# LSH attention and two mixture layers on one core: the attention result's halves added on GpSimd, v stored by partition, a new order

## The chip, the cores and the metric

One core of a Trainium2 chip runs the whole program in one launch. The metric is the device time in microseconds (us) of that launch. The core's engines are PE (TensorE: matrix products and transposes), DVE (VectorE), ACT (ScalarE) and POOL (GpSimd); SP (SyncE) here only issues transfers. Each engine works through its own instructions in the order in which the program lists them.

## What is computed

The reference, cut to what matters. There are 2 x 8 heads of 768 positions and 64 channels; the result of the attention (1536 x 512) goes through two further layers, all in float32.

```python
q_bucket = bits of (q @ proj > 0), 6 bits; k_bucket likewise
scores = q @ k.T / 8, and -1e9 where q_bucket != k_bucket
attn = exp(scores - max);  attn = attn / (sum + 1e-9)
x = attn @ v                        # heads side by side: 1536 x 512
x = ((x @ w1) * (x @ w2)) @ w3 @ w_out
p = domain_probs / (sum + 1e-9)
out = sum over 4 experts e of p[:, e] * (relu(x @ e1[e]) @ e2[e])
```

## The kernel before, in words

Every float32 operand of a product is split into a high and a low part of a narrower type (hi and lo), and three or four products of parts take the place of one.

**Attention.** The work is 48 units u: 16 heads hh of 3 blocks of 256 queries each. For a head, `head` loads q and k (`ld`), scales and splits them on POOL (`sc`, `h`, `l`; for the first two heads on ACT and DVE), and sends pieces between partitions by transfers issued from SP (`k1`, `k2`, `k3`, `dq`). `lv` loads v, `vh` and `vl` split it on POOL. `pair` (and `first_head` for head 0) makes the mask bits: a product on PE (`bm`), a comparison on DVE, and transfers `mq` and `mk` that put them beside q and k.

A unit (`unit`) goes through every engine: scores of two blocks of 128 queries on PE (`S`); minimum with its copy out of PSUM on DVE (`mx`); exponential on ACT (`ex`); sum plus 1e-9 on POOL (`r1`), reciprocal on DVE (`r2`), scaling on POOL, one in four on ACT (`en`); then three groups of four transposes on PE (`T`), each copied out as a high part by ACT (`hi`) and a low part by DVE (`lo`); then twelve products with v on PE (`pv`) into one bank, pv_ps. Its 128 partitions hold two halves of 64 (products with the high and with the low part of v) that are to be added. Before the change ACT copies the lower half into `pvs` (`po`, line 502) and DVE adds it to the upper half in PSUM (`xa`, line 504) into xt, and the next unit's `pv` may then begin.

**Weights.** Weights come in 64-bit words. `conv64` (line 176) loads one, ACT and DVE turn it to float32 and split it; the first 8 pieces run beside the attention, with the last steps on POOL.

**The first product in attention.** The product of x's first 512 rows with w1 and w2 has 8 column tiles `ff` of twice 12 products. FILL of them (4 before) are put into gaps of PE in the late attention (`fm`; from unit UF = 38 on they have the bank `f_ps`, one group of twelve uses s_ps). After `switch` the memory is given to the later layers, and the rest of the first product and everything else run on PE as one long row of products (`u_ps`, `o_ps`).

**What sets the order.** No loop sets it. Each step is an `op` with an engine, an assumed duration in ns, the steps it waits for and a priority; `emit_all` plays a list scheduler over these: when an engine falls free in its model it takes the ready op with the smallest priority, and a finished op reaches another engine after LAT. Priority is the due time plus RANK of the group times 5500. The order that comes out is written as each engine's instruction list. The chip runs these lists with its own durations, and every list in order: an instruction whose input is late holds up all behind it on that engine. For SP the assumed duration stands for a transfer's place on the queue, and LAT of SP for its landing.

Of the kernel before, what the change touches and what calls it, by code (L numbers as in the profile page):

```python
# [14 lines left out]
ALU = mybir.AluOpType  # L15
# [11 lines left out]
    "CP": 16.1,  # L27
    "S0": -59.56,
    "S1": 3.69,
    "T0": -207.42,  # L30
    "T1": -82.6,
    "T2": -31.6,
    "b0": -57.56,
    "b1": -59.96,
    "bits": -7.65,
    "en": 2.75,
    "ex0": -95.56,
    "ex1": -444.49,
    "fd": -89.32,
    "fx": 240.7,  # L40
    "hi0": -7.87,
    "hi1": -248.41,
    "hi2": -157.19,
    "ld": -54.46,
    "lo0": -345.82,
    "lo1": -186.61,
    "lo2": -153.95,
    "lv": -53.81,
    "mx0": -264.79,
    "mx1": -0.59,  # L50
    "p0": -157.78,
    "p1": -422.6,
    "po": -405.44,
    "prep": 73.11,
    "pv": -5.01,
    "r1": -199.11,
    "r2": -270.42,
    "v": 180.48,
    "xa": -317.88,
}  # L60
# [11 lines left out]
def tile_lsh_attention_moe(ctx, tc, qk, v, projc, w1, w2, w3T, w_out, dp, e1, e2, out):  # L72
# [15 lines left out]
    def tiles(n, shape, name, dtype=F32, p=None):  # L88
        return [(p or ap).tile(shape, dtype, name=f"{name}{i}") for i in range(n)]
# [7 lines left out]
    NE_SLOTS = 4  # L97
    FILL = 4
    slots = [const.tile([128, 2, 1024], F32R, name=f"slot{i}") for i in range(NE_SLOTS)]
# [78 lines left out]
    def conv64(n, dst, half, src):  # L178
        r = raws[n % NRAW]

        def hi_():
            return slots[dst][:, 0, half * 512:(half + 1) * 512]

        def lo_():
            return slots[dst][:, 1, half * 512:(half + 1) * 512]

        ri = r.bitcast(I32)
        lw, hw = (ri.rearrange("p (a b) -> p a b", b=2)[:, :, i] for i in range(2))
        c, t = cbuf[:, n % NCB, 0], cbuf[:, n % NCB, 1]
        beside = n < NBESIDE  # L190
        side, sdur, seng, minus = ("POOL", 1225, nc.gpsimd, pool_lo) if beside else ("DVE", 620, nc.vector, lo_of)
        return [
            ("SP", 1460, [("cd", n - NRAW), ("c2", n - NRAW)], "cl",
             lambda: nc.sync.dma_start(out=ri.rearrange("p (a b) -> p a b", a=src.shape[1]), in_=src)),
            ("ACT", 520, [("cl", n), ("cq", n - NCB)], "ca",
             lambda: nc.scalar.activation(out=f(c), in_=f(hw), func=AF.Abs)),
            ("DVE", 335, [("ca", n)], "c0",
             lambda: nc.vector.tensor_scalar(out=f(c), in0=f(c), scalar1=EXP_LO, scalar2=EXP_HI, op0=ALU.max, op1=ALU.min)),
            ("DVE", 335, [("c0", n)], "c1",
             lambda: nc.vector.tensor_scalar(out=t, in0=c, scalar1=3, scalar2=0x3FFFFFFF, op0=ALU.logical_shift_left,  # L200
                                             op1=ALU.bitwise_and)),
            ("DVE", 602, [("c1", n)], "c2",
             lambda: nc.vector.scalar_tensor_tensor(out=c, in0=hw, scalar=-0x40000000, in1=t, op0=ALU.bitwise_and,  # L203
                                                    op1=ALU.bitwise_or)),
            ("DVE", 335, [("c2", n)], "c3",
             lambda: nc.vector.tensor_scalar(out=t, in0=c, scalar1=-0x800000, scalar2=None, op0=ALU.bitwise_and)),  # L206
            ("ACT", 520, [("c2", n)], "ch",
             lambda: nc.scalar.activation(out=hi_(), in_=f(c), func=AF.Copy)),
            (side, sdur, [("ch", n)], "cp", lambda: minus(lo_(), f(c), hi_())),
            ("DVE", 602, [("c3", n)], "cd",  # L210
             lambda: nc.vector.scalar_tensor_tensor(out=f(t), in0=lw.bitcast(U32), scalar=2.0 ** -52, in1=f(t),  # L211
                                                    op0=ALU.mult, op1=ALU.mult)),
            (side, sdur, [("cp", n), ("cd", n)], "cq",
             lambda: seng.tensor_tensor(out=lo_(), in0=f(lo_()), in1=f(t), op=ALU.add)),
        ]
# [17 lines left out]
    def conv(n, dst, half, src):  # L233
# [95 lines left out]
    def head(hh):  # L329
# [10 lines left out]
        def load(part):  # L340
            nc.sync.dma_start(out=r[part], in_=qk[b, h, part])
# [4 lines left out]
        def scaled_lo(eng):  # L346
            eng.scalar_tensor_tensor(out=lo, in0=r, scalar=svec, in1=f(hi), op0=ALU.mult, op1=ALU.subtract)
# [12 lines left out]
        else:  # L360
            op(("ld", hh), "SP", 1130, lambda: load(slice(0, 2 * D)), [("l", hh - RR)] if hh >= RR else [],
               -1e9 + 1e7 * hh if first else T - 8000)
            if first:
                op(("h", hh), "ACT", 733, lambda: nc.scalar.activation(out=hi, in_=r, func=AF.Copy, scale=svec),
                   [("ld", hh), ("sv", 0)], T, g)
# [6 lines left out]
            op(("k1", hh), "SP", 700, lambda: copy(ka[q], hi[k]), [("h", hh)] + old, T, g)  # L372
            op(("k3", hh), "SP", 700, lambda: copy(kb[q], hi[k]), [("h", hh)] + old, T, g)
            op(("k2", hh), "SP", 700, lambda: copy(ka[k], lo[k]), [("l", hh)] + old, T, g)
            op(("dq", hh), "SP", 700, lambda: copy(hi[k], hi[q]),
               [("bm", hh // 2 if hh > 1 else 0), ("k1", hh), ("k3", hh)], T, g)
# [45 lines left out]
    def unit(u):  # L422
# [6 lines left out]
        for t in range(2):  # L429
# [22 lines left out]
        def norm(t):  # L452
# [43 lines left out]
        Tp = T + 2.0 * P  # L496
        pvs = pvs_t[u % 2]
# [401 lines left out]
```

## Time and profile before

| | |
|---|---|
| median of 3 runs | 1017.81 us (1017.12 to 1022.36) |
| the profiled execution: its own time | 1020.02 us |
| its span, first to last instruction | 1018.2 us |
| busy: PE, DVE, ACT, POOL | 999.7, 510.1, 362.5, 307.8 us |
| bytes moved | 64.12 MB in 51135 packets, 17688 of them under 512 B |

The busy share of PE is 98%, but the profile models the ends of products, which overlap, so a busy PE is not PE at its peak. The span falls into two: the attention, in which all four engines work and hand on to one another, and what follows, in which PE runs products back to back. An engine that is nearly always busy in a stretch bounds it; an average over the span says nothing of that, so the prediction reads the stretches apart.

### The profile page before, as it was taken

What the parts mean: (1) busy time and instruction counts of PE and PEld (TensorE: products, weight loads), DVE (VectorE), ACT (ScalarE), POOL (GpSimd) and SP (SyncE); (2) the same over time, 40 slices, a digit from 0 to 9 for tenths busy, and PEclk for the clock granted to TensorE, in tenths of its full rate; (3) what the DMA queues carried; (4) which work ended last, traced back from release to release, by engine and by line L of the source; (5) the groups of instructions that cost most, each with busy time, mean ns of one, the idle gap of its engine ahead of it and who ended that gap; (6) DMA issues with size and microseconds to landing.
All of it is one profiled execution on the core that took longest, in us unless ns stands there. A gap on an engine that the chain in (4) does not pass through costs nothing.

```text
span 1018.2 us, 13166 instructions
## 1 busy us (share of the span) xinstructions
PE 999.7 (98%) x5035; PEld 844.6 (83%) x5035; DVE 510.1 (50%) x948; ACT 362.5 (36%) x669; POOL 307.8 (30%) x351
## 2 busy tenths in 40 slices
PE   7899999999999999999999999999999999999998
PEld 6888888988788888888888888888888888888886
DVE  6889999998599965954312212121121212212122
ACT  5889999988433322432201101101101101101100
POOL 6777788664000000074300064000650005300000
PEclk9999999999999999999999999999999999999999
DMA  6843544320034321332200032000220002001011
GB/s 162 184 128 77 130 121 112 82 80 21 1 116 127 119 94 49 117 103 63 63 1 1 1 93 73 0 1 1 78 88 1 1 1 73 31 1 42 1 42 42
DMA packets 51135, 64.12 MB, mean 63 GB/s; under 512 B 17688, under 2 KB 34072, under 8 KB 51072
## 3 DMA queue, kind: packets, MB, share of 16 engines
q1 hardware_dynamic: 50928, 63.27, 22.0%
q8 instruction: 40, 0.66, 0.3%
q14 instruction: 23, 0.19, 0.1%
q10 hardware_dynamic: 144, 0.01, 0.0%
HBM read 47.22 MB, written 3.15 MB: 49 GB/s over the span
## 4 chain that ended last, share of the span: by engine, by line
PE 82%; DVE 14%; DMA 1%; ACT 1%; issue 1%; POOL 1%; SPq 0%; DVEq 0%; ACTq 0%; POOLq 0%
PE u_ps L147 43%; PE o_ps L147 30%; DVE et L485 5%; DVE e L443 5%; PE s_ps L147 3%; PE pv_ps L147 2%; PE t_ps L477 2%; PE t_ps L147 2%; DVE xa L504 1%; DVE cbuf L211 1%; DMA wraw<-in_w 1%; ACT e L446 1%; DMA kb<-hh 0%; DVE cbuf L203 0%; DVE cbuf L206 0%
## 5 line engine op out<-in xcount | busy, mean ns | idle before, releaser
L819 DVE SCALAR_TENSOR_TENSOR hl<-u_ps,hl 128x512 fp32r<-128x512 f32 x96 | 66.4, 691 | 420.4 <-ACT hl L817 420.4
L817 ACT ACTIVATE hl<-u_ps 128x512 fp32r<-128x512 f32 x96 | 57.4, 598 | 459.3 <-PE u_ps L147 401.9
L147 PE MATMUL u_ps<-xh,slotl 128*128 128x512 f32 x936 | 220.6, 389 | 0.0
L147 PEld LDWEIGHTS u_ps<-xh,slotl 128*128 128x128 f32 x936 | 175.7, 188 | 36.5
L147 PE MATMUL u_ps<-xh,slot 128*128 128x512 f32 x696 | 165.0, 389 | 1.2 <-DVE xh L156 1.2
L147 PE MATMUL o_ps<-slotl,hl 128*128 128x512 f32 x648 | 154.7, 389 | 0.0
L147 PEld LDWEIGHTS u_ps<-xh,slot 128*128 128x128 f32 x696 | 130.6, 188 | 28.7 <-DVE xh L156 1.6
L147 PEld LDWEIGHTS o_ps<-slotl,hl 128*128 128x128 f32 x648 | 121.6, 188 | 25.2
L147 PE MATMUL o_ps<-slot,hl 128*128 128x512 f32 x504 | 119.9, 389 | 0.0
L147 PEld LDWEIGHTS o_ps<-slot,hl 128*128 128x128 f32 x504 | 94.6, 188 | 19.6
L159 POOL TENSOR_SCALAR slot<-wraw 128x512 fp32r<-128x512 f32 x28 | 17.8, 634 | 286.7 <-PE u_ps L147 269.7
L485 DVE TENSOR_TENSOR et<-t_ps,et 128x512 fp32r<-128x512 f32 x144 | 96.6, 680 | 5.8 <-ACT et L483 5.2
L446 ACT ACTIVATE e<-e,sm 128x768 f32<-128x768 f32 x96 | 89.5, 933 | 12.3 <-DVE e L443 11.0
L147 PE MATMUL pv_ps<-et,vv 128*128 128x256 f32 x576 | 92.8, 297 | 0.8 <-DVE xa L504 0.5
L443 DVE TENSOR_SCALAR_CACHE_REDUCE e<-s_ps 128x768 f32<-128x768 f32 x96 | 90.4, 945 | 4.9 <-PE t_ps L477 3.0
L477 PE MATMUL t_ps<-ident,e 128*128 128x128 f32 x576 | 87.0, 279 | 5.7 <-DVE et L485 4.0
L483 ACT ACTIVATE et<-t_ps 128x512 fp32r<-128x512 f32 x144 | 83.0, 592 | 12.5 <-PE t_ps L477 5.7
L159 POOL TENSOR_SCALAR slotl<-wraw 128x512 fp32r<-128x512 f32 x36 | 22.5, 624 | 208.8 <-PE u_ps L147 172.3
L477 PEld LDWEIGHTS t_ps<-ident,e 128*128 128x128 f32 x576 | 66.3, 142 | 15.9 <-DVE et L485 8.5
L147 PEld LDWEIGHTS pv_ps<-et,vv 128*128 128x128 f32 x576 | 76.0, 192 | 3.0 <-DVE xa L504 2.4
L456 POOL TENSOR_SCALAR e<-e,sm 128x768 f32<-128x768 f32 x72 | 65.5, 916 | 17.4 <-DVE sm L461 15.4
L147 PE MATMUL s_ps<-ka,hh 128*128 128x512 f32 x192 | 53.5, 360 | 3.8 <-issue 2.2
(111 smaller groups left out, 1092.9 us busy)
## 6 DMA issues: line engine op xcount, KB each, us to landing
wraw<-in_e SPq DMA_DIRECT2D x64, 256.0 KB
wraw<-in_w SPq DMA_DIRECT2D x16, 512.0 KB
wraw<-in_w3T SPq DMA_DIRECT2D x16, 512.0 KB
r<-in_qk SPq DMA_DIRECT2D x15, 384.0 KB
wraw<-in_w_out SPq DMA_DIRECT2D x8, 512.0 KB
rv<-in_v SPq DMA_DIRECT2D x16, 192.0 KB
out<-xa SPq DMA_DIRECT2D x12, 256.0 KB
ka<-hh SPq DMA_DIRECT2D x15, 192.0 KB
```

The source lines that it names most:

```text
L147: nc.tensor.matmul(out=o, lhsT=l, rhs=r, start=start, stop=stop)
L159: nc.gpsimd.tensor_scalar(out=o, in0=i, scalar1=1.0, scalar2=1.0, op0=ALU.mult, op1=ALU.mult)
L211: lambda: nc.vector.scalar_tensor_tensor(out=f(t), in0=lw.bitcast(U32), scalar=2.0 ** -52, in1=f(t), op0=ALU.mult, op1=ALU.mult)),
L443: op(("mx", u, t), "DVE", 873, lambda ps=ps, m=m, e=e: nc.vector.tensor_scalar(out=e, in0=ps[:, 0:S], scalar1=THR, scalar2=None, op0=ALU.m ...
L446: op(("ex", u, t), "ACT", 921, lambda e=e, m=m, rs=rs: nc.scalar.activation(out=e, in_=e, func=AF.Exp, scale=-1.0, bias=m, accum_out=rs), ...
L456: return "POOL", 872, lambda: nc.gpsimd.tensor_scalar(out=e, in0=e, scalar1=r[:, t:t + 1], scalar2=1.0, op0=ALU.mult, op1=ALU.mult)
L477: nc.tensor.transpose(out=ps[:, k, t * 128:(t + 1) * 128], in_=e_t[2 * (u % ER) + t][:, kt * 128:(kt + 1) * 128], identity=ident)
L483: op(("hi", n), "ACT", 480, lambda ps=ps, et=et: nc.scalar.activation(out=et[:, 0], in_=ps, func=AF.Copy), [("T", u, j), ("pv", n - NET)], Tj)
L485: op(("lo", n), "DVE", 602, lambda ps=ps, et=et: nc.vector.tensor_tensor(out=et[:, 1], in0=ps, in1=f(et[:, 0]), op=ALU.subtract), [("hi", ...
L504: op(("xa", u), "DVE", 340, lambda: nc.vector.tensor_tensor(out=xt[a, h // 2, t0:t0 + 256], in0=pv_ps[0:D], in1=pvs, op=ALU.add), [("po", ...
L817: op(("gh", n), "ACT", 480, lambda n=n, nu_=nu_: nc.scalar.activation(out=hl_t[n % 2][:, 0], in_=u_ps[nu_ % 4], func=AF.Relu), [ku] + hfre ...
L819: op(("uf", nu_), "DVE", 602, lambda n=n, nu_=nu_: nc.vector.scalar_tensor_tensor(out=hl_t[n % 2][:, 1], in0=u_ps[nu_ % 4], scalar=0.0, in ...
```

## The change

Five things change, all of them within the attention, and the order with them.

- `po` copies all 128 partitions of pv_ps into `pvs` (three buffers now). A transfer from SP (`pm`, new) puts one half of it into `pvd` on the partitions of the other half, and POOL, no longer DVE, adds the two (`xa`). The next unit's `pv` waits for `po`, no longer for `xa`.
- v lies in memory with 1.5 KB in a row for a partition, so that its load is 128 rows of 1.5 KB and no longer 768 of 256 B.
- For head 0 the comparison for q is cut in two: 256 columns, which unit 0 needs, then the other 512 (`sf`). `l` of head 1 now waits for the first of these.
- FILL is 2, no longer 4.
- All values of RANK are new, assumed durations are changed (transfers of weights 2700, no longer 1460; of q and k 2000, no longer 1130; copies 1000, no longer 700; conversions some 15% longer), and LAT of SP is 1900, no longer 2300. The load of head 2 also waits for the copies of head 0.

```diff
 RANK = {
...
-    "b0": -57.56,
+    "b0": -203.5,
...
-    "mx0": -264.79,
-    "mx1": -0.59,
-    "p0": -157.78,
-    "p1": -422.6,
-    "po": -405.44,
+    "mx0": -137.39,
+    "mx1": -120.26,
+    "p0": -518.7,
+    "p1": -224.16,
+    "pm": -94.42,
+    "po": -345.53,
...
-    "xa": -317.88,
+    "xa": -90.07,
 }
...
-    FILL = 4
+    FILL = 2
...
-    pvs_t = tiles(2, [64, 256], "pvs")
+    pvs_t = tiles(3, [128, 256], "pvs")
+    pvd_t = tiles(2, [128, 256], "pvd")
...
-            ("SP", 1460, [("cd", n - NRAW), ("c2", n - NRAW)], "cl",
+            ("SP", 2700, [("cd", n - NRAW), ("c2", n - NRAW)], "cl",
...
-        "SP": {"PE": 2300, "ACT": 2300, "DVE": 2300, "POOL": 2300, "SP": 2300, "NONE": 0},
+        "SP": {"PE": 1900, "ACT": 1900, "DVE": 1900, "POOL": 1900, "SP": 1900, "NONE": 0},
...
-            op(("ld", hh), "SP", 1130, lambda: load(slice(0, 2 * D)), [("l", hh - RR)] if hh >= RR else [],
+            op(("ld", hh), "SP", 2000, lambda: load(slice(0, 2 * D)), [(x, hh - RR) for x in (("l", "k1", "k2", "k3", "dq") if hh == RR else ("l",))],
...
-                op(("l", hh), "DVE", 870, lambda: scaled_lo(nc.vector), [("h", hh)], T, g)
+                op(("l", hh), "DVE", 1000, lambda: scaled_lo(nc.vector), [("h", hh), ("mq", 0)], T, g)
...
-        op(("lv", hh), "SP", 600, lambda: nc.sync.dma_start(out=rv, in_=v[b, h].rearrange("(k p) d -> p k d", p=128)),
+        op(("lv", hh), "SP", 1000, lambda: nc.sync.dma_start(out=rv, in_=v[b, h].rearrange("p (k d) -> p k d", k=NK)),
...
-        op(("mq", 0), "DVE", 865, lambda: is_pos(lo[64:64 + PC], ps, q), [("mk", 0)], T, "b0")
-        keys[("sf", n)] = keys[("mq", 0)]
+        for i, (key, c) in enumerate(((("mq", 0), slice(0, 256)), (("sf", n), slice(256, S)))):
+            op(key, "DVE", (330, 600)[i], lambda c=c: is_pos(lo[64:64 + PC, c], ps, q, c), [("mk", 0)], T + i, "b0")
...
-            op(("pv", n), "PE", 472, lambda j=j: pv(j), [("lo", n), ("vl", hh), ("xa", u - 1), ("pv", n - 1)], Tp)
+            op(("pv", n), "PE", 472, lambda j=j: pv(j), [("lo", n), ("vl", hh), ("po", u - 1), ("pv", n - 1)], Tp)
...
-        op(("po", u), "ACT", 264, lambda: nc.scalar.activation(out=pvs, in_=pv_ps[D:2 * D], func=AF.Copy),
-           [("pv", NJ * u + NJ - 1), ("xa", u - 2)], Tp)
-        op(("xa", u), "DVE", 340, lambda: nc.vector.tensor_tensor(
-            out=xt[a, h // 2, t0:t0 + 256], in0=pv_ps[0:D], in1=pvs, op=ALU.add), [("po", u)], Tp)
+        w, t0 = h % 2, b * S + qp * 256
+        a, o = slice(w * D, (w + 1) * D), slice((1 - w) * D, (2 - w) * D)
+        op(("po", u), "ACT", 283, lambda: nc.scalar.activation(out=pvs, in_=pv_ps, func=AF.Copy),
+           [("pv", NJ * u + NJ - 1), ("xa", u - 3)], Tp)
+        op(("pm", u), "SP", 500, lambda: nc.sync.dma_start(out=pvd[a], in_=pvs[o]), [("po", u), ("xa", u - 2)], Tp)
+        op(("xa", u), "POOL", 520, lambda: nc.gpsimd.tensor_tensor(
+            out=xt[a, h // 2, t0:t0 + 256], in0=pvs[a], in1=pvd[a], op=ALU.add), [("pm", u)], Tp)
```

## Rows read from the trace of the kernel before

**Rows 1.** Windows view: span, then PE, PEld, DVE, ACT, POOL busy (instructions), clock, DMA share, GB/s.
```profile
50.00:250.00 200.00, 194.21 (x1376) 175.72 (x1375) 193.39 (x408) 181.06 (x358) 145.34 (x174) 0.99 0.39 96
...
262.70:272.96 10.26, 10.26 (x45) 8.18 (x44) 1.11 (x2) 3.73 (x8) 0.00 (x0) 1.00 0.00 0
272.96:1018.20 745.24, 740.30 (x3265) 612.50 (x3263) 269.75 (x441) 135.60 (x228) 124.30 (x128) 1.00 0.15 49
```

**Rows 2.** Groups of instructions of DVE, 50 to 250 us: busy us, mean ns, idle before.
```profile
L485 DVE TENSOR_TENSOR et<-t_ps,et 128x512 fp32r<-128x512 f32 x120 | 80.5, 679 | 2.7 <-ACT et L483 2.3
L443 DVE TENSOR_SCALAR_CACHE_REDUCE e<-s_ps 128x768 f32<-128x768 f32 x80 | 75.4, 945 | 1.3 <-PE s_ps L147 0.9 <-PE t_ps L477 0.4
L504 DVE TENSOR_TENSOR xa<-pv_ps,pvs 64x256 f32<-64x256 f32 x40 | 16.5, 412 | 1.4 <-ACT pvs L502 0.7
L211 DVE SCALAR_TENSOR_TENSOR cbuf<-wraw,cbuf 128x512 f32<-128x512 uint32 x8 | 8.4, 1055 | 0.0
```

**Rows 3.** The last step of the weight conversion, whole span: ns min/median/max.
```profile
L211 DVE SCALAR_TENSOR_TENSOR cbuf<-wraw,cbuf x40: 672/692/1440, 60.9 to 434.8; 128x512 f32<-128x512 uint32 x40
```

**Rows 4.** Groups of instructions of POOL, 50 to 250 us.
```profile
L162 POOL TENSOR_TENSOR ll<-r,hh 128x768 fp32r<-128x768 f32 x10 | 18.4, 1840 | 0.7
L162 POOL TENSOR_TENSOR vv<-rv,vv 128x384 fp32r<-128x384 f32 x13 | 13.2, 1013 | 0.9
...
L159 POOL TENSOR_SCALAR vv<-rv 128x384 fp32r<-128x384 f32 x13 | 6.6, 510 | 4.5 <-PE pv_ps L147 4.2
```

**Rows 5.** Groups of instructions of ACT, two copies that differ in partitions alone.
```profile
L358 ACT ACTIVATE hh<-r,svec 64x768 fp32r<-64x768 f32 x1 | 0.9, 936 | 1.4 <-POOL ka L162 1.4
L352 ACT ACTIVATE hh<-r,svec 128x768 fp32r<-128x768 f32 x1 | 0.9, 935 | 0.1
```

**Rows 6.** Waits in 50 to 250 us: total, times, longest.
```profile
PEld pv_ps L147 <- DVE xa L504: 2.1, 4, 0.8
```

**Rows 7.** Timeline of the start: start us, us, what, idle before.
```profile
6.03 2.60 POOL L162 TENSOR_TENSOR ka<-r,hh 64x768 fp32r<-64x768 f32 x1 [4.24 <-ACT hh L352]
...
7.28 2.17 DVE L347 SCALAR_TENSOR_TENSOR ll<-r,svec,hh 128x768 fp32r<-128x768 f32 x1 [0.34 <-ACT hh L364]
...
7.57 0.28 PE L147 MATMUL s_ps<-ll,pbh 128*128 128x256 f32 x1
...
9.48 1.07 DVE L394 TENSOR_SCALAR kb<-s_ps,thr,amp 12x768 fp32r<-12x768 f32 x1
...
10.59 1.07 DVE L394 TENSOR_SCALAR ll<-s_ps,thr,amp 12x768 fp32r<-12x768 f32 x1
...
12.37 0.96 DVE L443 TENSOR_SCALAR_CACHE_REDUCE e<-s_ps 128x768 f32<-128x768 f32 x1 [0.71 <-PE s_ps L147]
```

**Rows 8.** Line 347 (`l` of heads 0 and 1): ns min/median/max.
```profile
L347 DVE SCALAR_TENSOR_TENSOR ll<-r,svec,hh x2: 1018/1594/2169, 5.9 to 7.3; 128x768 fp32r<-128x768 f32 x2
```

**Rows 9.** Timeline of a weight load and the first step that reads it.
```profile
61.60 0.37 SPq L194 DMA_DIRECT2D wraw<-in_w  x1
...
67.87 0.67 ACT L196 ACTIVATE cbuf<-wraw 128x512 f32<-128x512 f32 x1 [2.66 <-DMA wraw<-in_w]
```

**Rows 10.** Timeline where the attention ends.
```profile
262.69 0.38 ACT L502 ACTIVATE pvs<-pv_ps 64x256 f32<-64x256 f32 x1 [2.12 <-PE pv_ps L147]
...
272.96 0.39 PE L147 MATMUL u_ps<-xh,slot 128*128 128x512 f32 x1
...
274.57 7.76 PE L147 MATMUL u_ps<-xh,slot 128*128 128x512 f32 x33 [1.22 <-DVE xh L156]
```

**Rows 11.** The chain that ended last, a piece of the later layers.
```profile
299.79 99.96 PE u_ps L147 x441
```

**Rows 12.** What POOL's steps on rv waited for (total, times); no transfer is listed.
```profile
  PE pv_ps L147: 7.0, 4
```

More of the change, by code (lines that the diff above doesn't have):

```diff
@@ L27 @@
     "CP": 16.1,
[L28 to L32, printed above, removed]
-    "b0": -57.56,
[L34 to L48, printed above, removed]
-    "mx0": -264.79,
-    "mx1": -0.59,
-    "p0": -157.78,
-    "p1": -422.6,
-    "po": -405.44,
[L54 to L58, printed above, removed]
-    "xa": -317.88,
+    "S0": -22.24,
+    "S1": 34.2,
+    "T0": -375.86,
+    "T1": 1.27,
+    "T2": 12.38,
+    "b0": -203.5,
+    "b1": -262.95,
+    "bits": -145.66,
+    "en": -212.23,
+    "ex0": 51.78,
+    "ex1": -67.51,
+    "fd": -58.23,
+    "fx": -3.38,
+    "hi0": -121.05,
+    "hi1": -521.6,
+    "hi2": -135.75,
+    "ld": -100.06,
+    "lo0": -161.12,
+    "lo1": -345.51,
+    "lo2": -121.56,
+    "lv": -1.34,
+    "mx0": -137.39,
[4 more added lines that the diff above has]
+    "po": -345.53,
+    "prep": -14.07,
+    "pv": 35.79,
+    "r1": -204.44,
+    "r2": -334.47,
+    "v": -45.12,
+    "xa": -90.07,
 }
@@ L190, in conv64 @@
         beside = n < NBESIDE
-        side, sdur, seng, minus = ("POOL", 1225, nc.gpsimd, pool_lo) if beside else ("DVE", 620, nc.vector, lo_of)
+        side, sdur, seng, minus = ("POOL", 1290, nc.gpsimd, pool_lo) if beside else ("DVE", 620, nc.vector, lo_of)
         return [
-            ("SP", 1460, [("cd", n - NRAW), ("c2", n - NRAW)], "cl",
+            ("SP", 2700, [("cd", n - NRAW), ("c2", n - NRAW)], "cl",
              lambda: nc.sync.dma_start(out=ri.rearrange("p (a b) -> p a b", a=src.shape[1]), in_=src)),
-            ("ACT", 520, [("cl", n), ("cq", n - NCB)], "ca",
+            ("ACT", 570, [("cl", n), ("cq", n - NCB)], "ca",
              lambda: nc.scalar.activation(out=f(c), in_=f(hw), func=AF.Abs)),
-            ("DVE", 335, [("ca", n)], "c0",
+            ("DVE", 400, [("ca", n)], "c0",
              lambda: nc.vector.tensor_scalar(out=f(c), in0=f(c), scalar1=EXP_LO, scalar2=EXP_HI, op0=ALU.max, op1=ALU.min)),
-            ("DVE", 335, [("c0", n)], "c1",
+            ("DVE", 400, [("c0", n)], "c1",
              lambda: nc.vector.tensor_scalar(out=t, in0=c, scalar1=3, scalar2=0x3FFFFFFF, op0=ALU.logical_shift_left,
                                              op1=ALU.bitwise_and)),
-            ("DVE", 602, [("c1", n)], "c2",
+            ("DVE", 700, [("c1", n)], "c2",
              lambda: nc.vector.scalar_tensor_tensor(out=c, in0=hw, scalar=-0x40000000, in1=t, op0=ALU.bitwise_and,
                                                     op1=ALU.bitwise_or)),
-            ("DVE", 335, [("c2", n)], "c3",
+            ("DVE", 400, [("c2", n)], "c3",
              lambda: nc.vector.tensor_scalar(out=t, in0=c, scalar1=-0x800000, scalar2=None, op0=ALU.bitwise_and)),
@@ L209, in conv64 @@
             (side, sdur, [("ch", n)], "cp", lambda: minus(lo_(), f(c), hi_())),
-            ("DVE", 602, [("c3", n)], "cd",
+            ("DVE", 700, [("c3", n)], "cd",
              lambda: nc.vector.scalar_tensor_tensor(out=f(t), in0=lw.bitcast(U32), scalar=2.0 ** -52, in1=f(t),
@@ L360, in head @@
         else:
-            op(("ld", hh), "SP", 1130, lambda: load(slice(0, 2 * D)), [("l", hh - RR)] if hh >= RR else [],
+            op(("ld", hh), "SP", 2000, lambda: load(slice(0, 2 * D)), [(x, hh - RR) for x in (("l", "k1", "k2", "k3", "dq") if hh == RR else ("l",))],
                -1e9 + 1e7 * hh if first else T - 8000)
             if first:
-                op(("h", hh), "ACT", 733, lambda: nc.scalar.activation(out=hi, in_=r, func=AF.Copy, scale=svec),
+                op(("h", hh), "ACT", 830, lambda: nc.scalar.activation(out=hi, in_=r, func=AF.Copy, scale=svec),
                    [("ld", hh), ("sv", 0)], T, g)
-                op(("l", hh), "DVE", 870, lambda: scaled_lo(nc.vector), [("h", hh)], T, g)
+                op(("l", hh), "DVE", 1000, lambda: scaled_lo(nc.vector), [("h", hh), ("mq", 0)], T, g)
             else:
@@ L371, in head @@
                 op(("l", hh), "POOL", 1800, lambda: pool_lo(lo, r, hi), [("h", hh)] + old, T, g)
[L372 to L375, printed above, removed]
+            op(("k1", hh), "SP", 1000, lambda: copy(ka[q], hi[k]), [("h", hh)] + old, T, g)
+            op(("k3", hh), "SP", 1000, lambda: copy(kb[q], hi[k]), [("h", hh)] + old, T, g)
+            op(("k2", hh), "SP", 1000, lambda: copy(ka[k], lo[k]), [("l", hh)] + old, T, g)
+            op(("dq", hh), "SP", 1000, lambda: copy(hi[k], hi[q]),
                [("bm", hh // 2 if hh > 1 else 0), ("k1", hh), ("k3", hh)], T, g)
@@ L391, in bits_of, with is_pos @@
                 mm(ps[:, r], pbh[:, a, :], lo[:, r], False, i == len(hs) - 1)
-    def is_pos(dst, ps, r):
-        nc.vector.tensor_scalar(out=dst, in0=ps[r, 0:S], scalar1=thr[r], scalar2=amp[r], op0=ALU.is_gt, op1=ALU.mult)
+    def is_pos(dst, ps, r, c=slice(0, S)):
+        nc.vector.tensor_scalar(out=dst, in0=ps[r, c], scalar1=thr[r], scalar2=amp[r], op0=ALU.is_gt, op1=ALU.mult)
     def first_head():
@@ L441, in unit @@
             Tt = T + t * P / 2
-            op(("S", u, t), "PE", 690, score, [(k, hh) for k in ("mq", "mk", "k1", "k2", "k3", "dq")] + free_, Tt)
+            op(("S", u, t), "PE", 690, score, [(k, hh) for k in ("mq", "mk", "k1", "k2", "k3", "dq")] +
+               ([("sf", 0)] if 0 < u < NQ else []) + free_, Tt)
             op(("mx", u, t), "DVE", 873, lambda ps=ps, m=m, e=e: nc.vector.tensor_scalar(
@@ L457, in norm @@
                 out=e, in0=e, scalar1=r[:, t:t + 1], scalar2=1.0, op0=ALU.mult, op1=ALU.mult)
-        op(("r1", u), "POOL", 300, lambda: nc.gpsimd.tensor_scalar(
+        op(("r1", u), "POOL", 295, lambda: nc.gpsimd.tensor_scalar(
             out=sm[:, 0:2], in0=sm[:, 6:8], scalar1=1e-9, scalar2=None, op0=ALU.add), ex, T + 2 * P)
@@ L496, in unit @@
         Tp = T + 2.0 * P
[L497 removed]
+        pvs, pvd = pvs_t[u % 3], pvd_t[u % 2]
         for j in range(NJ):
             n = NJ * u + j
[L500 removed]
+            op(("pv", n), "PE", 472, lambda j=j: pv(j), [("lo", n), ("vl", hh), ("po", u - 1), ("pv", n - 1)], Tp)
         a, t0 = slice((h % 2) * D, (h % 2 + 1) * D), b * S + qp * 256
[L502 to L505 removed]
+        w, t0 = h % 2, b * S + qp * 256
[5 more added lines that the diff above has]
+            out=xt[a, h // 2, t0:t0 + 256], in0=pvs[a], in1=pvd[a], op=ALU.add), [("pm", u)], Tp)
     def zero_consts():
```

4 lines of the change are left out of this document (2 added, 2 removed).

## The prediction, made before the change had run

> **What bounds the kernel now.** I read the windows first, because the span has two parts with different limits. After the attention, 745.2 us of the 1018.2, PE is busy for 740.3 us and the other engines have room [rows 1]; a chain of 441 products there takes 99.96 us, 0.227 us each [rows 11]. The change takes no product out of this part, so the time must come from the attention. There, in the 200 us from 50 to 250, DVE is busy for 193.4 us, 96.7%; ACT for 181.1, POOL for 145.3. PE reads 194.2, but its weight loads are busy for 175.7 only, so it is less full than it looks [rows 1]. The reader should see two things: DVE bounds this stretch, and ACT and PE stand close behind it. Next I read what DVE does there: the copies out of PSUM (80.5 and 75.4 us) are most of it; the sum of the halves is 40 instructions, 16.5 us [rows 2]. Then the two ends of the stage: the start, a chain of single steps in which no engine is full [rows 7], and the end, where PE runs 45 products of the first layer after the attention's last one [rows 1, 10].
>
> **The sum taken off DVE.** Removed from DVE in the 200 us: 40 adds, 16.5 us [rows 2], which leaves 176.9. ACT's copy now has 128 partitions for 64; two copies that differ in this alone took 936 and 935 ns [rows 5], so it costs nothing, and ACT keeps 181.1: it is the next bound. The next unit's products wait for the copy and no longer for the add; the weight loads waited 2.1 us for that, four times [rows 6], which lies inside what follows and is not added.
>
> POOL receives 40 adds of 256 columns. The trace has none of this size. Two-input steps of POOL took 1840 ns for 768 columns and 1013 for 384 [rows 4]: 827 ns for 384 columns more, and on this line 1013 - 128 x 827/384 = 0.74 us for 256. Lower end: 0.51, a one-input step of 384 columns; upper end: 1.01, the two-input step of 384 columns [rows 4]. I take 0.74, since the rows of the same operation are the nearest. POOL then has 145.3 + 29.6 = 174.9 us (165.7 to 185.7), still under ACT.
>
> If ACT came to be as full as DVE was, the stretch would last 181.1/0.967 = 187.2 us, 12.8 less. But DVE at 176.9, weight loads at 175.7 and POOL at 174.9 would all stand within 7 us of it, and four engines that wait for one another seldom fill the first of them. The other end is no gain. I take the middle, **-6.4 us** (0 to -12.8).
>
> Each unit also issues one transfer on SP. An issue there takes about 0.4 us [rows 9], so 40 are some 16 us of SP's time, on which nothing else computes. But the transfer waits for the copy, and everything behind it on SP's list (loads of later heads, copies between partitions, mask bits) waits with it; those are issued heads ahead, which is the cover. If that cover is gone, scores wait for a head's copies. On POOL the add waits for the landing, and behind it stand the 1e-9 sums, which DVE's reciprocals need, and the scalings, which the transposes need. The trace bounds the landing from one side: the weight load issued at 61.60 was read at 67.87, 6.3 us later [rows 9], with a load eight times as large. The order assumes 0.5 + 1.9 = 2.4 us. Three copies of pvs and two of pvd let an add come a unit late without stopping PE. In the sum I set these waits at 0; a rival below has their price.
>
> DVE steps with two SBUF inputs are slowed where POOL works: line 211 took 1055 ns on average in the attention [rows 2] against 692 as the median of the whole span [rows 3], 8 x 0.36 = 2.9 us in all. POOL's 29.6 us more, a fifth of what it does now, would add some 0.6 us; the two large groups of DVE, which read PSUM, are not of this kind. This is less than the room on DVE (176.9 under 181.1) and goes into the range. The Trainium skill (Perfetto Trace Analysis, section Optimizing Scalar/DVE Operations) speaks against the move: GpSimd and DVE share an SBUF read port, so shifting work between the two might not help. The trace agrees for line 211; for the PSUM readers no row shows it. By the row the sum stays as it is; by the rule, taken for all of DVE, it would be the last rival below.
>
> **The start.** Now the comparison for k starts at 9.48, though its product ended at 7.57 + 0.28 = 7.85; DVE was held by line 347 from 7.28 to 9.45 [rows 7]. Line 347 now waits until q's first 256 columns are compared. Then k runs from about 7.9 to 9.0, q's 256 columns to about 9.4 (a third of 1.07 us and something for the fixed part), the rest to about 10.2. What goes next on DVE? Line 347, 1.02 us if POOL lets it, as in its other execution, or 2.17 as here [rows 8], where POOL ran from 6.03 to 8.63 beside it [rows 7]. So the first `mx` begins at 11.2 to 12.3, instead of 12.37; at about 10.1 if the order puts line 347 behind it. Between -0.1 and -2.3 I take **-0.9**, the case of the undisturbed line 347 with something kept back, because head 1's low part comes some 2 us later than now. That is needed only when head 1's scores begin; without this slack it would give the gain back.
>
> **The corrected durations.** The order expects a weight piece 1.46 + 2.3 = 3.8 us after its issue; it took 6.3, and ACT stood 2.66 us for it [rows 9]. The new order expects 4.6, that is 0.8 later: **-0.8** for this wait (0 to -2.7). Other such misfits I cannot price; they are in the middle value above.
>
> **The first product and the switch.** 48 products go from the attention to the row behind it and cost 48 x 0.227 = 10.9 us there. Before, 45 ran after the last product of the attention [rows 1], so 51 ran inside it; the 48 that are left fit into the same gaps. Work of PE after the attention's last product changes by +48 - 45 = 3 products, +0.7 us. After the switch PE now waits 1.22 us for DVE's split of x [rows 10]. Two column tiles of block 0 are then ready without any split, and 10.9 us of work cover it: -1.2. Together **-0.5**, between -1.2 and +2.2 (if one group of twelve, which must wait for a bank of the scores, 2.7 us, is left over). Two more pairs of copies go behind the switch on ACT and DVE; the 10.9 us that PE is busy there cover them.
>
> **v in longer rows: 0.** POOL's steps on v waited for PE's products and never for the load [rows 12]. Without that cover the load of 192 KB would be late by at most its own time.
>
> The sum is -6.4 - 0.9 - 0.8 - 0.5 = -8.6 us. Against the profiled execution's own 1020.0 us (span 1018.2) that gives 1011.4; the median of the runs is 2.2 us below that execution, so the forecast is 1017.8 - 8.6 = **1009.2**. All best ends together give -19.0, all worst ends +2.1.
>
> **Rivals.** *The pace stays.* POOL at its upper price has 185.7 us, more than ACT; with two engines over 90% and an order that is new in every rank, waits take the place of DVE's bound, and only the small terms remain: 1017.8 - 2.2 = 1015.6. For it: ACT already stands at 181.1 of 200. Against: DVE at 96.7% shows that an order can fill one engine. Chance 0.24.
>
> *ACT gets as full as DVE was*: 1017.8 - 12.8 - 2.2 = 1002.8. For it: DVE, in an order of the same kind, left only 6.6 us of the 200 idle. Against: four engines within 7 us. Chance 0.20.
>
> *POOL waits for the transfers* (slower). The place is POOL's list, the add at its head and the 1e-9 sums behind it. POOL has 200 - 174.9 = 25.1 us to spare in 40 units, so a mean wait over 0.63 us decides. At 0.9 us POOL needs 174.9 + 36 = 210.9 us, 10.9 more than the stretch has now: 1017.8 + 10.9 - 2.2 = 1026.5. For it: a landing took 6.3 us behind other loads, and the order assumes 2.4. Against: the order now counts large loads as longer, and buffers allow a unit of delay. Chance 0.12.
>
> *POOL's adds stop DVE* (slower): if DVE stood for all 29.6 us of them, it would need 176.9 + 29.6 = 206.5 us, at 96.7% a stretch of 213.5, so 1017.8 + 13.5 - 2.2 = 1029.1. For it: line 211. Against: 156 of DVE's 193 us read PSUM, and kept a steady 679 and 945 ns with POOL 73% busy [rows 1, 2]. Chance 0.04. The rule of the Trainium skill named above would lead here.
>
> **How the numbers follow.** The forecast's own case has 0.40. A difference of about 0.5%, 5.1 us, is what a measurement of this kernel can tell from no change. Faster by more: the forecast and the fuller ACT, 0.60. Within: the pace that stays, 0.24. Slower: the last two, 0.16. The range 1000 to 1021 leaves out the best third of the second rival (0.06) and most of the two slow ones (0.13). The forecast's own case alone reaches from 1004 to 1012.7.
>
> **What would show it.** In the profile after: no DVE add on xa, 48 POOL adds near 0.74 us; in a stretch of the middle attention DVE at 90 to 94% and ACT the fullest; the first `mx` near 11.5; 48 instead of 96 first-layer products in the attention, almost none after its last own product, and no wait behind the switch. The attention's last copy of pv_ps, now at 262.7 [rows 10], should come near 254.6 (the first three terms). I am wrong if POOL shows long idle times that end with a transfer into pvd, if DVE stays over 96%, or if ACT waits as long as before in sum.

## The result, and the profile after

The changed kernel took 1027.67 us (median of 5 runs, 1025.61 to 1028.07) against 1017.4 before: the ratio is 1.0082, 95% interval [1.0056, 1.0107]. It is slower; the forecast was 1009.2, with a range up to 1021.0. The profiled execution took 1025.61 us, its span is 1023.8; the profiled execution of before (1020.02) lay above its median and this one below, so the two profiles differ by 5.6 us in span where the medians differ by 10.3.

The windows of the changed kernel, cut at its own marks (columns as in [rows 1]; 260.8 is its last copy of pv_ps, 265.1 its first product behind the switch):

```profile
50.00:250.00 200.00, 184.74 (x1309) 166.40 (x1309) 189.33 (x359) 171.32 (x348) 175.17 (x210) 0.99 0.40 106
...
260.80:265.10 4.30, 4.30 (x21) 3.56 (x19) 0.00 (x0) 2.91 (x6) 1.08 (x2) 1.00 0.46 137
265.10:1023.80 758.70, 752.38 (x3313) 621.13 (x3311) 273.58 (x443) 137.36 (x231) 123.83 (x129) 1.00 0.15 48
```

In the same 200 us PE made fewer products (1309 for 1376) and ACT did less (171.3 for 181.1). POOL has 175.2 us, as worked out (174.9). But DVE, which has lost its 40 adds, is busy for 189.3 us and not for 176.9. The groups of DVE in this stretch tell why; first after, then the four lines of before that the rows above do not show (198, 200, 203 and 206 are now 200, 202, 205 and 208):

```profile
L488 DVE TENSOR_TENSOR et<-t_ps,et 128x512 fp32r<-128x512 f32 x116 | 76.1, 678 | 1.3 <-ACT et L486 1.0
L446 DVE TENSOR_SCALAR_CACHE_REDUCE e<-s_ps 128x768 f32<-128x768 f32 x77 | 72.1, 944 | 0.0
L213 DVE SCALAR_TENSOR_TENSOR cbuf<-wraw,cbuf 128x512 f32<-128x512 uint32 x8 | 12.5, 1559 | 0.0
L200 DVE TENSOR_SCALAR cbuf<-cbuf 128x512 f32<-128x512 f32 x8 | 9.4, 1178 | 0.0
L208 DVE TENSOR_SCALAR cbuf<-cbuf 128x512 int32<-128x512 int32 x8 | 8.8, 1104 | 0.0
L202 DVE TENSOR_SCALAR cbuf<-cbuf 128x512 int32<-128x512 int32 x8 | 6.9, 864 | 0.0
L205 DVE SCALAR_TENSOR_TENSOR cbuf<-wraw,cbuf 128x512 int32<-128x512 int32 x8 | 6.9, 862 | 0.0
```
```profile
L203 DVE SCALAR_TENSOR_TENSOR cbuf<-wraw,cbuf 128x512 int32<-128x512 int32 x7 | 5.8, 824 | 0.1
L206 DVE TENSOR_SCALAR cbuf<-cbuf 128x512 int32<-128x512 int32 x8 | 5.4, 675 | 0.0
L198 DVE TENSOR_SCALAR cbuf<-cbuf 128x512 f32<-128x512 f32 x7 | 3.7, 545 | 0.0
L200 DVE TENSOR_SCALAR cbuf<-cbuf 128x512 int32<-128x512 int32 x7 | 2.9, 418 | 0.0
```

The two big groups, which read PSUM, kept their 678 and 944 ns. The five steps of the weight conversion read and write SBUF alone; together they took 44.5 us for 40 steps. Before it was 26.2 us for 37, which makes 28.1 for 40 at the same means. Line 213 (211 before) went from 1055 [rows 2] to 1559 ns. The adds themselves, and what waited for POOL, in the groups of POOL and the waits of the same stretch, the last line from before:

```profile
L510 POOL TENSOR_TENSOR xa<-pvs,pvd 64x256 f32<-64x256 f32 x39 | 29.2, 750 | 5.7 <-DMA pvd<-pvs 3.4
```
```profile
DVE sm L464 <- POOL sm L462: 9.0, 13, 1.4
PEld t_ps L480 <- POOL e L459: 8.1, 14, 1.3
PEld t_ps L480 <- POOL sm L462: 6.7, 4, 2.2
```
```profile
PEld t_ps L477 <- POOL e L456: 0.6, 2, 0.4
```

DVE's reciprocals waited 9.0 us for POOL's sums (at most 0.5 before), and the transposes 8.1 us for its scalings (0.6 before). Landings hold POOL for 3.4 us in this stretch, and for 6.1 us more at the end of the attention.

By units (a unit is counted at its copy of pv_ps): unit 8 came at 65.0 us (before 74.6), units 8 to 14 took 30.1 us (28.7), units 14 to 34 took 106.6 us (95.3), units 34 to 47 took 59.1 us (64.1), and the last copy came at 260.8 (262.7). So the new order gained 9.6 us at the start and lost 12.7 in the middle. The 5.0 us after unit 34 are no clear gain: fewer products of the first layer stood in the gaps there. 20 of 48 still ran after the attention's last own product, so 28 ran inside where 51 had; 23 products are 5.2 us at 0.227 us each, and they are paid behind the attention. The row of products behind the switch begins 7.9 us earlier (265.1 for 273.0) and lasts 13.5 us longer (758.7 for 745.2), 10.9 of it for the 48 products that were moved there. That makes the 5.6 us between the two profiles.

### The profile page after: what moved, and what is told of

Read it like the earlier page. It is cut to its first block, busy times and chain, and to the rows that moved or that the text cites. A ratio compares the mean times of both kernels' runs of the same rounds, so it can differ in the third digit from the quotient of the medians.

```text
span 1023.8 us, 13349 instructions
## 1 busy us (share of the span) xinstructions
PE 998.0 (97%) x5035; PEld 842.7 (82%) x5035; DVE 509.2 (50%) x901; ACT 356.1 (35%) x669; POOL 344.9 (34%) x399
## 4 chain that ended last, share of the span: by engine, by line
PE 86%; DVE 6%; POOL 3%; ACT 2%; issue 2%; DMA 1%; DVEq 0%; POOLq 0%; ACTq 0%
PE u_ps L149 44%; PE o_ps L149 30%; PE s_ps L149 5%; PE pv_ps L149 4%; PE t_ps L480 4%; DVE et L488 1%; DVE e L446 1%; POOL e L459 1%; PE t_ps L149 1%; DVE cbuf L213 1%; POOL xa L510 1%; DVE cbuf L208 1%; DVE cbuf L200 1%; ACT e L449 0%; ACT et L486 0%
## 5 line engine op out<-in xcount | busy, mean ns | idle before, releaser
L149 PE MATMUL u_ps<-xh,slot 128*128 128x512 f32 x744 | 175.9, 389 | 1.2 <-DVE xh L158 1.2
L149 PEld LDWEIGHTS u_ps<-xh,slot 128*128 128x128 f32 x744 | 139.6, 188 | 30.6 <-DVE xh L158 1.6
L480 PE MATMUL t_ps<-ident,e 128*128 128x128 f32 x576 | 84.2, 277 | 14.9 <-DVE et L488 10.8
L488 DVE TENSOR_TENSOR et<-t_ps,et 128x512 fp32r<-128x512 f32 x144 | 94.7, 680 | 6.0 <-ACT et L486 5.6
L149 PE MATMUL pv_ps<-et,vv 128*128 128x256 f32 x576 | 90.2, 293 | 0.0
L486 ACT ACTIVATE et<-t_ps 128x512 fp32r<-128x512 f32 x144 | 82.1, 593 | 14.4 <-PE t_ps L480 9.6
L459 POOL TENSOR_SCALAR e<-e,sm 128x768 f32<-128x768 f32 x72 | 68.3, 957 | 9.9 <-DVE sm L464 5.2
```

Of the source, the lines that this page charges most:

```text
L149: nc.tensor.matmul(out=o, lhsT=l, rhs=r, start=start, stop=stop)
L459: return "POOL", 872, lambda: nc.gpsimd.tensor_scalar(out=e, in0=e, scalar1=r[:, t:t + 1], scalar2=1.0, op0=ALU.mult, op1=ALU.mult)
L480: nc.tensor.transpose(out=ps[:, k, t * 128:(t + 1) * 128], in_=e_t[2 * (u % ER) + t][:, kt * 128:(kt + 1) * 128], identity=ident)
L486: op(("hi", n), "ACT", 480, lambda ps=ps, et=et: nc.scalar.activation(out=et[:, 0], in_=ps, func=AF.Copy), [("T", u, j), ("pv", n - NET)], Tj)
L488: op(("lo", n), "DVE", 602, lambda ps=ps, et=et: nc.vector.tensor_tensor(out=et[:, 1], in0=ps, in1=f(et[:, 0]), op=ALU.subtract), [("hi", ...
```

## The experiments

**Undoing or doing one part.** In the runs of this part (e1 to e4, e7, e8, e11, e12) the scheduler makes new lists for each.

Run e1: `FILL = 4` in the changed kernel.

> The changed kernel with FILL 4 in place of 2, all else as changed. The row of products behind the attention lasted 758.7 us in the changed kernel against 745.2 before, 48 x 0.227 = 10.9 of it moved there, while the attention itself took 28 first-layer products in its gaps and not 51. Theory that FILL 2 costs: the gaps take more products again, about 7 us less than the changed kernel, near 1020. Rival (the gaps of the new order are too small for more, so each product left over runs behind the attention all the same): within 2 us of the changed kernel, 1026 to 1029, with some 68 products after the attention's last one.

1028.43 us, ratio to the kernel before 1.0099 [1.0069, 1.0128]; 68 products ran after the attention's last one and the row behind was 747.9 us. The rival holds: FILL is not the loss, the gaps of the new order take no more products.

Run e4: `FILL = 2` in the kernel before.

> The kernel before with FILL 2 alone. Theory that FILL 2 costs by itself: 48 products (10.9 us) go behind the attention, the gaps lose some of what they took, and the two later waits of 0.85 us appear there: 1021 to 1026. Rival (as predicted: 48 still fit in the gaps and the wait behind the switch goes): 1016 to 1018.

1018.77 us, 1.0008 [0.9995, 1.0022]. All 48 ran inside the attention, the first product behind it came at 264.0 in place of 273.0, and the row there grew by 10.0 us. FILL moves work from one place of PE's list to another; a difference over some 2 us is not seen.

Run e2: the changed kernel with the sum on DVE as before.

```diff
-        op(("pm", u), "SP", 500, lambda: nc.sync.dma_start(out=pvd[a], in_=pvs[o]), [("po", u), ("xa", u - 2)], Tp)
-        op(("xa", u), "POOL", 520, lambda: nc.gpsimd.tensor_tensor(
-            out=xt[a, h // 2, t0:t0 + 256], in0=pvs[a], in1=pvd[a], op=ALU.add), [("pm", u)], Tp)
+        op(("po", u), "ACT", 283, lambda: nc.scalar.activation(out=pvs, in_=pv_ps[D:2 * D], func=AF.Copy),
...
+        op(("xa", u), "DVE", 340, lambda: nc.vector.tensor_tensor(
+            out=xt[a, h // 2, t0:t0 + 256], in0=pv_ps[0:D], in1=pvs, op=ALU.add), [("po", u)], Tp)
```

> The changed kernel with the halves summed on DVE out of PSUM as before (no transfer, no POOL add, the next unit's products wait for the sum); new ranks, durations, v rows, mask bits and FILL 2 stay. Theory that POOL is what slows the middle (its adds fill its list and block DVE's conversion steps): the 20 units from 14 to 34, 106.6 us in the changed kernel, go back to some 97, conversion steps back to about 1.0 us for line 213's, total near 1018. Rival (the new order itself is worse, whoever adds): DVE is loaded with 16.5 us again and the total rises over 1030.

1043.7 us, 1.0249 [1.0223, 1.0275], the range of the rival; units 14 to 34 took 119.2 us. The conversion steps fell to 29.7 us, but DVE was only 90.7% busy between units 8 and 34 (96.7% in the changed kernel): with the sum back on its list it waited more.

Run e3: the kernel before with `pm`, POOL's add and the buffers of the change.

> The kernel before with one part of the change alone: transfer and POOL add for the halves, three and two buffers, the products wait for the copy; ranks, durations and FILL stay (the transfer has the rank of the copy). Theory that POOL slows the middle: 20 units from 14 to 34 take 103 us or more against 95.3, total 1022 to 1030. Rival (relief of DVE helps and the ranks spoil it): those units take 92 or less, total under 1012.

1047.2 us, 1.0286 [1.0259, 1.0312], but not in the way expected. Units 14 to 34 took 94.3 us. The loss was at one place: PE stood 12 us for POOL's low part of v, and units 8 to 14 took 51.7 us for 28.7. The rank of v's split puts it late (180.48; -45.12 in the changed kernel), and POOL's list had grown.

Run e7: the same with `"v": -45.12`.

> The kernel before with the halves summed by transfer and POOL, and one rank changed besides: that of the splitting of v, from 180.48 to -45.12, the value that the changed kernel has. With the old rank the same kernel took 1047.2 and stood 12 us at one place, PE's products with v behind POOL's low part of v (line 164). Theory that the 29 us there were mostly this one misplaced step: that wait goes, total 1015 to 1025. Rival (POOL's list is too full in any order): another wait takes its place, total over 1035.

1042.13 us, 1.023 [1.0213, 1.0247]: that wait went and others came (unit 8 at 87.0), the rival. Runs e2, e3 and e7 say one thing together: ranks fit one set of steps. A part that is moved alone pays for new lists, and its own price can't be read from that.

Run e8: the mask bits alone, new lists. Run e12: the new durations alone. Run e11: `NBESIDE = 0` in the changed kernel.

> The kernel before with the mask bits of head 0 moved up and cut in two, nothing else. In the changed kernel the first minimum began at 11.0 in place of 12.37. Theory that this is a gain of its own: first minimum at 11 to 11.5, total 1 to 2 us less than before, 1016 to 1017. Rival (head 1's low part, 2 us later, gives it back, or the order of the rest shifts): 1017 to 1025.

> The kernel before with the changed assumed durations, the changed landing time of SP and the changed waits of the load of head 2, old ranks, nothing else. In the changed kernel unit 8 left PE's products at 65.0 in place of 74.6 us. Theory that the corrected durations bring this: unit 8 at 70 or earlier, total 1005 to 1013. Rival (old ranks belong to old durations, or the new ranks bring it): unit 8 later than 72, total 1017 or more.

> The changed kernel with the last two steps of the first 8 weight pieces on DVE in place of POOL (NBESIDE 0): 16 steps, 21 us less on POOL, 16 x 0.69 = 11 us more on DVE. Theory that POOL's list and the shared use of SBUF bound the middle: POOL falls to some 82% there, total 1012 to 1022. Rival (DVE at 96.7% cannot take more): 1032 or more. The order of the lists is made anew and can move it either way.

e8: 1031.58 us, 1.0125 [1.0109, 1.0141], first minimum at 14.4, later than before, and the total over both ranges. e12: 1030.98 us, 1.0116 [1.0099, 1.0133], unit 8 at 73.3, the rival. e11: 1024.98 us, 1.0054 [1.0037, 1.0071]; POOL fell to 83% and units 14 to 34 took 106.4 us all the same. e11 is in neither theory's range and settles nothing. e12 shows that the corrected durations don't bring the early gain with the old ranks.

**The changed lists, one instruction exchanged.** The following runs keep the scheduler's input and change only what the add's `op` puts out, so every list stays in the order of the changed kernel.

Run e5: no add.

```diff
-        op(("pm", u), "SP", 500, lambda: nc.sync.dma_start(out=pvd[a], in_=pvs[o]), [("po", u), ("xa", u - 2)], Tp)
-        op(("xa", u), "POOL", 520, lambda: nc.gpsimd.tensor_tensor(
-            out=xt[a, h // 2, t0:t0 + 256], in0=pvs[a], in1=pvd[a], op=ALU.add), [("pm", u)], Tp)
+        op(("pm", u), "SP", 500, lambda: nc.sync.dma_start(out=xt[a, h // 2, t0:t0 + 256], in_=pvs[o]), ...
+        op(("xa", u), "POOL", 520, lambda: None, [("pm", u)], Tp)
```

> The changed kernel with every instruction list in the same order, but POOL's 48 adds are left out: the transfer writes its half into xt itself, so that the other half is missing from the sum. Theory that POOL's adds are what slows the middle of the new order (35 us of POOL's list, its waits for transfers, and DVE's conversion steps blocked beside them): units 14 to 34 from 106.6 us to 97 or less, conversion steps on DVE from 44.5 us to 30 or less, total 1012 or less. Rival (the new lists are badly ordered whatever POOL adds): units 14 to 34 stay over 103, total over 1021.

1009.03 us, 0.9902 [0.9886, 0.9919]; units 14 to 34 took 95.9 us. The theory that the adds are the cost holds: they cost 1027.67 - 1009.03 = 18.6 us (18.3 by the ratios to the kernel before, which was run beside each). Conversion steps fell to 34.0 us, less far than expected: of the growth from 28.1 to 44.5 us, 10.5 come with the adds, and 5.9 are there without them.

Run e6: each add twice.

> The changed kernel, same order of the lists, each of POOL's adds made twice (36 us more on POOL). Theory that POOL's list is what bounds the middle: at 91.7% busy it has little left, so most of the second add is paid, 20 to 33 us more than the changed kernel, 1048 to 1060, and the conversion steps grow by another 10 us or so. Rival (POOL is not on the path, waits lie elsewhere): less than 8 us more.

1051.23 us, 1.0315 [1.0299, 1.033]: 23.6 us more for the second 36 us of adds. About half of an add's time is paid (18.6/36 for the first, 23.6/36 for the second). The expected 10 us more of conversion did not come: 46.9 us for 39 steps, after 44.5 for 40. DVE's waits for POOL's sums rose instead, from 9.0 to 21.2 us, which points to POOL's list as the place where the second add is paid.

Run e9: three `memset`s of spare tiles, together as long as an add, in its place; they wait for nothing. Run e10: `in1=pvs[a]`, so that the add waits for no transfer.

> The changed kernel, lists in the same order; in place of each of POOL's adds stand three fills of a spare tile with zeros (256, 256 and 16 columns, 0.31 + 0.31 + 0.1 us, as long as an add), which read no SBUF and wait for no transfer; the transfer writes into xt itself and one half is missing from the sum. Leaving the adds out had saved 18.6 us (1009.0 against 1027.7). Theory of the list (time and place on POOL's list are the price): 1022 to 1028. Theory of the port (adds that read two SBUF operands block DVE's conversion steps and are blocked by them): conversion steps near 34 us as without adds, total 1009 to 1014.

> The changed kernel, lists in the same order; POOL adds the half that is already there to itself, so that no add waits for its transfer (it is still issued, and one half is missing from the sum). Theory that waiting for landings is what costs (POOL's adds stood idle 12.7 us before they began): 1014 to 1019. Rival (landings lie under other waits, the adds' own time costs): 1024 to 1028, units 14 to 34 still over 103 us.

e9: 1014.44 us, 0.9955 [0.9939, 0.9972], just above the range of the port theory, and the conversion steps as that theory had them. e10: 1022.9 us, 1.0041 [1.0027, 1.0056], units 14 to 34 105.0 us: between the two ranges, so waiting and the adds' own time both cost. The three longest of the five conversion lines, 50 to 250 us, first of e9, then of e10:

```profile
L213 DVE SCALAR_TENSOR_TENSOR cbuf<-wraw,cbuf 128x512 f32<-128x512 uint32 x8 | 8.4, 1053 | 0.0
L202 DVE TENSOR_SCALAR cbuf<-cbuf 128x512 int32<-128x512 int32 x8 | 7.9, 984 | 0.0
L200 DVE TENSOR_SCALAR cbuf<-cbuf 128x512 f32<-128x512 f32 x8 | 7.3, 910 | 0.0
```
```profile
L213 DVE SCALAR_TENSOR_TENSOR cbuf<-wraw,cbuf 128x512 f32<-128x512 uint32 x8 | 12.1, 1513 | 0.0
L200 DVE TENSOR_SCALAR cbuf<-cbuf 128x512 f32<-128x512 f32 x8 | 9.4, 1178 | 0.0
L208 DVE TENSOR_SCALAR cbuf<-cbuf 128x512 int32<-128x512 int32 x8 | 9.2, 1150 | 0.0
```

The other two lines add 5.9 and 5.3 us in e9 (743 and 668 ns), 6.4 and 6.2 us in e10 (795 and 771 ns). With fills that hold POOL as long as the adds did (POOL 173.2 us in this stretch, against 175.2), the five conversion steps take 34.9 us, nearly as with no adds; with adds that read SBUF they take 43.2.

So the 18.6 us fall into three steps. Time on POOL's list: 5.4 (1009.03 to 1014.44); DVE's waits for POOL's sums rose from 3.2 to 6.9 us. Fills exchanged for adds that read SBUF: 8.5 (to 1022.90), near the 8.3 us by which the conversion steps grew; in this stretch no wait of e10's adds for their copy is listed, so that difference between fill and add does not count there. The real add, which waits for the landing: 4.8 (to 1027.67; 4.2 by the ratios). The last step is the weakest. The two intervals touch at 1.0056, so it could be 1 us or 7; and an add of a tile to itself took 626 ns on average and the real one 747, 5.8 us over 48 adds. At half price that is 2.9 us, an estimate, so what the landing alone costs is not shown. The three are also not fixed prices: with a second add (e6) the conversion steps hardly grew and the list took the cost.

**Fewer and larger adds.** e13 and e14 keep the changed lists too. Two heads' halves are gathered by transfers and added together, 8 pieces of 128 x 512 and 8 of 128 x 256, in e13 on POOL (the diff), in e14 on DVE (`nc.vector` in the add). ACT copies the first head of a pair straight into xt.

```diff
+        def move():
+            if w:
+                nc.sync.dma_start(out=pvd[D:2 * D, c0:c0 + 256], in_=pvs[0:D])
+                nc.sync.dma_start(out=x[D:2 * D], in_=pvs[D:2 * D])
+            else:
+                nc.sync.dma_start(out=pvd[0:D, c0:c0 + 256], in_=x[D:2 * D])
+        def sums():
+            if w and qp:
+                c = slice(0, 512) if qp == 1 else slice(512, S)
+                xs = xt[:, h // 2, b * S + c.start:b * S + c.stop]
+                nc.gpsimd.tensor_tensor(out=xs, in0=xs, in1=pvd[:, c], op=ALU.add)
+        op(("po", u), "ACT", 283, lambda: nc.scalar.activation(out=pvs if w else x, in_=pv_ps, func=AF.Copy),
```

> The changed kernel, lists in the same order, but the halves of two heads are gathered by transfers (72 in place of 48) and added in 16 pieces on POOL, 8 of 128 x 512 and 8 of 128 x 256, about 16 us in place of 36. Theory that the adds' cost goes with their time on POOL: 16/36 of 18.6 is 8 us over the kernel without adds (1009.0), about 1017, some 10 us under the changed kernel; fewer waits for transfers. Rival (cost by something else, such as the transfers): over 1023.

> As the run before, but the 16 pieces are added on DVE, at the place that they have in the order as it was made: 8 x 0.69 and 8 x 0.4, about 9 us in place of the 19.8 us that DVE had before the change. Theory that DVE is the bound of this order when POOL adds nothing (99.2% busy in units 8 to 34 without adds): 9 us over 1009, 1018. If DVE also waits for transfers in its list: 1020 to 1028. Rival (DVE has room): 1012 or less.

e13: 1015.7 us, 0.9969 [0.9957, 0.998]. e14: 1014.19 us, 0.9956 [0.9942, 0.9969]. Both are faster than both kernels, by little. The sum costs 6.7 us on POOL and 5.2 on DVE over e5. e13 came as the theory had it, and its conversion steps stand at 35.0 us, near the 34.0 without adds. e14 is in no range of its expectation: DVE had more room than the theory said and less than the rival. The groups of DVE in e14 show the pieces; they too read SBUF alone, and are longer than the expected 690 and 400 ns:

```profile
L521 DVE TENSOR_TENSOR xa<-xa,pvd 128x512 f32<-128x512 f32 x8 | 7.8, 980 | 1.4 <-DMA xa<-pvs 1.4
...
L521 DVE TENSOR_TENSOR xa<-xa,pvd 128x256 f32<-128x256 f32 x8 | 4.1, 507 | 2.7 <-DMA xa<-pvs 2.7
```

**Two parts alone, the lists of before.** Run e15: v in rows of 1.5 KB. Run e16: mask bits moved up and cut; line 347's step and its copy are issued behind them.

> The kernel before with v in rows of 1.5 KB, every list in the same order. Theory that the load of v is hidden: within 1 us of the kernel before. Rival (the 12288 packets of 256 B hold up the transfers beside them between 25 and 45 us): 2 us or more less.

> The kernel before with the mask bits of head 0 moved up ahead of head 1's low part and cut in two, every list otherwise in the same order as before. Theory that this is a gain of its own: first minimum near 11.0 in place of 12.37 and 1 to 1.5 us less in total. Rival (the stage is held by later steps, so the earlier start is lost by unit 8): first minimum earlier, total unchanged within 0.5 us.

e15: 1018.32 us, 1.0 [0.999, 1.0009]: nothing, as expected. e16: 1018.56 us, 1.0002 [0.9993, 1.0011], the rival. Its first minimum began at 11.22. The chain of waits of e16 shows what came next:

```profile
10.29 1.03 DVE ll L349
...
11.84 3.53 DMA r<-in_qk
...
15.46 0.91 POOL r L371
```

The load of head 3 takes the buffer that head 1's low part (line 349 here, 347 before) reads. It now waits until that is done, and POOL begins on it at 15.46. The first copy of pv_ps came at 29.0, in place of 27.3. In the changed kernel, with its new order, it came at 25.8.

## Why the prediction was wrong, step by step

**The bound was read rightly, and the sum is nearly right for a kernel without the adds.** "DVE bounds this stretch": e5, with neither engine adding, took 1009.03, and the forecast was 1009.2. That is partly chance. The gain was to come from the middle, and in e5 units 14 to 34 took 95.9 us against 95.3: the adds that are gone freed some 8 us of DVE there, but five weight pieces in place of three lay in that stretch, with 21.2 us of conversion steps for 10.5, and DVE was 99.2% busy between units 8 and 34. The gain lay in the first 8 units, and after unit 34, where fewer products of the first layer ran.

**The failed step is the sum taken off DVE, in the place where the adds arrive at POOL.** The size of the add was right (0.74 us; 0.750 measured), and so was POOL's busy time (175.2 for 174.9); ACT's wider copy was free (384 ns for 380). What I then did with the adds failed in three places, of which each has a run:
- "still under ACT", so the time on POOL's list was free. It cost 5.4 us (e9). Busy time under the bound was no room in a list that is worked in order: reciprocals and transposes stood behind it.
- "would add some 0.6 us" for conversion steps slowed beside POOL. It was 8.3 us, 8.5 of total (e9 to e10). I had scaled one line of five by POOL's share of busy time. Lines 198 to 206 of the same conversion, in the same view, are also SBUF alone, and I did not price them. Another 5.9 us were there without any adds (e5); what drew them out is not shown.
- "I set these waits at 0" for the landings: they and the longer time of the real add together cost some 4.8 us (e10 to the changed kernel); their shares stay open.

The rule that I named against the move, that GpSimd and DVE share an SBUF read port (Trainium skill, Perfetto Trace Analysis, section Optimizing Scalar/DVE Operations), agrees with the conversion steps: 34.9 us beside fills, 43.2 beside adds that read SBUF. By the 678 and 944 ns of the PSUM readers it does not hold for all of DVE. No run here shows the port itself.

**The rivals.** The outcome has the sign of the last two, which had 0.16 together, and neither is it; 1027.67 lying between their 1026.5 and 1029.1 says nothing for either. *POOL waits for the transfers*: the point at which it decides, 0.63 us for each add, was not reached (3.4 us for 39). *POOL's adds stop DVE*: right in kind, but for conversion steps, not for all of DVE. Each stood as one mechanism; the result is three smaller ones at once, which no case held. Of the three signs of being wrong, two did not come: DVE over 96% (it was 94.7%), and long idle times before the adds (3.4 us in five waits in the middle). The third came: ACT stood idle for 28.7 us of the 200, before for 18.9. And the last copy of pv_ps, forecast near 254.6, came at 260.8.

**The start**: forecast -0.9. The first minimum came as worked out (11.0; 11.2 in e16), and in e16 the total did not move. I wrote that head 1's low part "is needed only when head 1's scores begin". It also frees a load buffer. What the earlier start is worth in the new order is not shown.

**The corrected durations**: -0.8 is not shown. With the old ranks they cost 12 us (e12), through the new lists they make. Whether they gain with the new ranks stays open. Part of unit 8's 9.6 us is the profiled execution of before: in e15, with the same lists, unit 8 came at 70.2 and not at 74.6.

**FILL**: forecast -0.5; e4 measured no difference within some 2 us, which fits. The steps were not: in the changed kernel 28 and not 48 products ran inside, and the wait of 1.22 us behind the switch stayed, as the timeline shows:

```profile
266.71 0.50 PE L149 MATMUL u_ps<-xh,slot 128*128 128x512 f32 x1 [1.22 <-DVE xh L158]
```

The tiles that needed no split were not put first. Behind it came waits of PE that were not there before (`o_ps` for ACT's line 155, 0.7 us twice).

**v**: 0, as predicted.

## What to carry to other kernels

Work that leaves a full engine should be priced where it arrives: by its place in that engine's list, by what it waits for there, and by which of the neighbour's steps read the same memory; busy time under the bound was not a price here. Where a scheduler makes the order, a part of a change is measured with the lists held still, by changing only what one step puts out. And a small sum made often is better gathered first: 16 adds in place of 48, with 72 transfers for 48, turned this change from 0.8% slower to 0.3% faster on POOL, and 0.4% when DVE made them.

## What was not expected of the hardware

A POOL step that writes SBUF but reads none (memset) left DVE's conversion steps at 34.9 us (34.0 with nothing in its place), while POOL adds, shorter than the fills (0.63 for some 0.74 us), drew them to 43.2 us; with each add made twice (e6) they stood at 46.9 us for 39 steps. One-input DVE steps were drawn out as well (line 200 from 704 ns without adds in e5 to 1178, line 208 from 872 to 1104), and the longest execution of line 213 took 3192 ns for a median of 692:

```profile
L213 DVE SCALAR_TENSOR_TENSOR cbuf<-wraw,cbuf x40: 674/692/3192, 76.2 to 443.3; 128x512 f32<-128x512 uint32 x40
```

Not tried: whether the one-input and the two-input steps are held by the same thing.
